# Attention and max-out FFN in one kernel: when value loads start, what follows them, and where two output blocks stand

## Chip, cores and metric

The kernel runs on one core of a Trainium2 chip, in one launch. Its time is the device time in microseconds, and the median of several runs is what is compared. A core has a matrix engine (PE), a vector engine (DVE), an activation engine (ACT), a general engine (POOL, GpSimd) and a queueing engine (SP). POOL and SP issue most transfers, which 16 DMA engines carry out.

## The reference

Eight batches of eight heads, 576 positions, head width 64. The inputs are float32.

```python
scores = scale * np.matmul(q, k.transpose(0, 1, 3, 2))
scores = scores + bias.transpose(2, 0, 1)[None, :, :, :]     # by distance, 32 buckets
attn = np.exp(scores - np.max(scores, axis=-1, keepdims=True))
attn = attn / (np.sum(attn, axis=-1, keepdims=True) + 1e-09)
x = np.matmul(attn, v)                                       # then to 4608 tokens x 512
h = np.maximum(np.maximum(x @ w1, x @ w2), x @ w3)           # 512 -> 768
return h @ w_out                                             # 768 -> 512
```

## The kernel before

**Tiles.** A batch b is worked off in four head pairs hp (HP = 4), so (b, hp) names a step. The 576 positions are four tiles of 128 (KT = 4) and a tail of 64. Scores are computed with keys on the partitions: `key_scores` (sc) gives one key tile against 512 queries, `left_keys_rows` (sct) the tail keys, and `left_queries` (scq) the tail queries. ACT takes the exponential of each (L776) into e4 or el. DVE multiplies a band around the diagonal by the exponential of the bias (L770; L856 and L869 for the tails). `attend_rows` then multiplies e4 and el by the values vx (main part) and vt (tail) on PE, into the tile a, one step later: the attention of (b, 3) is done in (b+1, 0), and that of (b+1, 0), the first to use batch b+1's values, in (b+1, 1).

**FFN between the scores.** From batch 4 on (ROWS) each step also runs one stage of the FFN of an earlier chunk of 512 tokens: in hp 2, hp 3 and the next batch's hp 0 a pair of gate blocks, and in hp 1 the outputs. Such a product is written as `pair`: `rows(False, c0, c1)` makes the first pass over blocks c0 to c1, `rows(True)` the second, with the partition halves exchanged. A pair of matmuls on the two halves runs side by side. In `outputs`, each of the six blocks (FCH = 6) of the first pass reads one block of hT. The last two blocks, 4 and 5, come from the third gate of the last gate pair, whose maximum (L518 on DVE) is what `largest` issues.

**Order.** `inorder` keeps instructions in program order on their engine, so the order on PE is that in which the Python code issues them. The output step's `run` sets: first half of sct, psp blocks, second half of sct, further psp blocks, the maximum, sc of key tile 3 (`more_scores`), bands, `left` (scq), and the rest. sc, sct and scq take turns in two PSUM buffers (pool ps_s): each waits until the exponential of the one two places before it is done. The second half of sct waits on a semaphore until the first half is through (`first_rows_end`, `behind_rows`).

**Transfers.** POOL issues the loads of q, k and v, which convert float32 to bfloat16 on the way. SP issues the transposes of q and k for the next batch (`transposes`, ten of them, q and k alternating through key tiles 0 to 3 and the tail), those of the attention's result x_sb into xT (L970, five at the end of a batch), and the stores of results. Each queue is worked in order. In step (b, 2) the program issues the loads of batch b+1's values (`load_v`: four vx, two vt) and then, for b from 2 to 5, those of batch b+2's q and k (`load_qk`: eight main parts, three tails); the buffers of both alternate. `go_behind(loads, ins)` makes each of these loads wait for an instruction `ins`, here the landing of a transpose: `turned_qk[b + 1, 1, t]` is that of key tile t of batch b+1, and t = KT is the tail. For b = 4 and up, values wait for t = KT and q and k for t = KT - 1.

Of the kernel before, what the change touches and what calls it, by code (L numbers as in the profile page):

```python
# [39 lines left out]
def kernel(  # L40
# [13 lines left out]
    B, H, S, D = q.shape  # L54
# [8 lines left out]
    KT = 4  # L63
# [14 lines left out]
    loads = ctx.enter_context(tc.tile_pool(name="loads", bufs=2))  # L78
# [36 lines left out]
    vx = [const.tile([P, KT, H, VW], BF16, name=f"vx{i}") for i in range(2)]  # L115
# [4 lines left out]
    def act_copy(out_, in_):  # L120
        return inorder(nc.scalar.activation(out=out_, in_=in_, func=ACTF.Copy))  # L121

    def dve_copy(out_, in_):
        return inorder(nc.vector.tensor_copy(out_, in_))  # L124

    def other_banks(later, earlier):

        for a in later:
            for b in earlier:
                tc.declare_no_dep(a.ins, b.ins, reason="they read different PSUM banks")  # L130
# [10 lines left out]
    def main_part(src, b):  # L141
        return src[b, :, 0 : KT * P, :].rearrange("h (t p) d -> p t h d", p=P)

    def tail_part(src, b, h0, h1, par):
        return src[b, h0 + par : h1 : 2, KT * P : S, :].rearrange("h p d -> p h d")

    def in_turn(b, load):
        return inorder(load)

    def load_main(src, b, h0, h1, dst, t0=0, t1=KT):  # L150
        x = main_part(src, b)
        return [
            in_turn(b, nc.gpsimd.dma_start(out=dst[:, t, h0:h1, :], in_=x[:, t, h0:h1, :])) for t in range(t0, t1)  # L153
        ]
# [5 lines left out]
    def load_q_tail(b):  # L160
        dst = qtail[b % 2][0 : S - KT * P].rearrange("p g (h d) -> p (g h) d", h=2)
        return in_turn(b, nc.gpsimd.dma_start(out=dst, in_=q[b, :, KT * P : S, :].rearrange("h p d -> p h d")))

    def k_diag(b, par, h0, h1):
        return diag(ktail[b % 2], par, h0, h1)
# [4 lines left out]
    def load_tail(src, b, h0, h1, dst):  # L170
        return [
            in_turn(b, nc.gpsimd.dma_start(out=dst(b, par, h0, h1), in_=tail_part(src, b, h0, h1, par)))
            for par in range(2)
        ]

    def load_qk(b, behind=None):

        loads = []
        for t in range(KT):
            for src, dst in zip((q, k), batch[b]):  # L180
                loads.append(in_turn(b, nc.gpsimd.dma_start(out=dst[:, t], in_=main_part(src, b)[:, t])))  # L181
        loads.append(load_q_tail(b))
        for par in range(2):
            load = nc.gpsimd.dma_start(out=k_diag(b, par, 0, H), in_=tail_part(k, b, 0, H, par))
            loads.append(in_turn(b, load))
        go_behind(loads, behind)

    def go_behind(loads, behind):

        for load in loads if behind else ():  # L190
            tc.add_manual_dep(
                load.ins, behind.ins.name,
                mybir.DependencyInfo(mybir.DependencyClass.Sync, mybir.DependencyReason.DATA),
                reason="these loads go behind the transposes in line",
            )

    def load_v(b, h0, h1, behind=None):
        loads = load_main(v, b, h0, h1, vx[b % 2][:, :, :, 0:D])
        go_behind(loads + load_tail(v, b, h0, h1, v_diag), behind)

# [139 lines left out]
    def pair(n, operands, pool, tag, w=CH):  # L342


        box = []

        def rows(swap, c0=0, c1=n):
            if not swap and c0 == 0:
                box.append(pool().tile([P, 2, CH], F32, tag=tag, name="psp"))
            made = []  # L350
            for c in range(c0, c1):
                for par in range(2):
                    i = par ^ swap
                    lhsT, rhs = operands[i](slice(64 * par, 64 * par + 64), c)
                    made.append(mm(
                        box[0][:, i, 0:w], lhsT=lhsT, rhs=rhs, start=not swap and c == 0, stop=swap and c == n - 1,
                    ))
            if swap:
                behind_rows(made[0], box[1])
            elif c1 == n:  # L360
                box.append(first_rows_end())

        return lambda: box[0][:, :, 0:w], rows

    def ffn(t0, nt, last, tiled=False):
# [172 lines left out]
        def columns(j, c0, c1):  # L538
            return lambda r, cf: (hT[r, cf * nt + j * P : cf * nt + j * P + P], wo_bf[r, cf, c0:c1])

        def osb_tile():
            return osbp.tile([P, d_model], F32, tag="osb", name="osb")

        def put_later(j, osb):
            r0 = t0 + j * P
            stores.append(lambda: inorder(nc.sync.dma_start(out=out[r0 : r0 + P, :], in_=osb[:])))

        def halves(j):
            ps, rows = pair(FCH, [columns(j, c, c + QS) for c in (0, QS)], lambda: ps_f, "ff", QS)

            def end():
                rows(True)

                def put():
                    osb = osb_tile()
                    dve_copy(osb[:].rearrange("p (i c) -> p i c", i=2), ps())
                    put_later(j, osb)
                return put
            return lambda: rows(False), end
# [28 lines left out]
        def outputs():  # L588
            ps0, rows0 = pair(FCH, [columns(j, 0, d_model) for j in range(2)], lambda: ps_a, "a")

            def end0():
                rows0(True)
                osb = osb_tile()
                first = act_copy(osb[:], ps0()[:, 0, :])
                put_later(0, osb)

                def put():
                    osb = osb_tile()
                    other_banks([dve_copy(osb[:], ps0()[:, 1, :])], [first])
                    put_later(1, osb)  # L600
                return put

            begin1, end1 = halves(2)

            def run(more_scores, left, ahead, largest, bands, keys):
                end_keys = keys()
                rows0(False, 0, 2)
                end_keys()
                rows0(False, 2, KT)
                largest()  # L610
                more_scores()
                bands()
                left()
                rows0(False, KT)
                begin1()
                put = end0()
                ahead()
                put()
                end1()()

            run.keys_late = True
            return run, lambda: halves(3)
# [143 lines left out]
    def times_band(hp, e4, t, lo, hi, put=lambda x: x):  # L766
        lo, hi = max(lo, P * t - P), min(hi, P * t + 2 * P)
        if lo < hi:
            c0, c1 = BAND - (hi - P * t + P), BAND - (lo - P * t + P)
            put(nc.vector.tensor_tensor(  # L770
                out=e4[:, t, :, lo:hi], in0=e4[:, t, :, lo:hi],
                in1=hank[:, 2 * hp : 2 * hp + 2, c0:c1][:, :, ::-1], op=ALU.mult,
            ))
# [86 lines left out]
    def left_queries(hp, qT, kT, el):  # L860

        sc = ps_s.tile([P, 2, CH], F32, tag="sc", name="scq")
        turn_left_queries(qT, kT, [sc[:, par, 0 : KT * 64] for par in range(2)])
        eq = el[:, S:].rearrange("p (t h q) -> p h t q", t=KT, h=2)
        return exp(eq, sc[:, :, 0 : KT * 64].rearrange("p h (t q) -> p h t q", t=KT))
# [7 lines left out]
    divided, turned_qk = {}, {}  # L873
# [161 lines left out]
    def bands(hp):  # L1035
        for t in range(KT):
            times_band(hp, first_e[hp], t, 0, QS, inorder)
# [40 lines left out]
    behind, begun = [], []  # L1078
    for hp in range(HP):
# [9 lines left out]
        def keys():  # L1089
            left_keys(hp, qT, kT, el, QS, S)  # L1090
# [57 lines left out]
    for b, hp in [(b, hp) for b in range(1, B) for hp in range(HP)]:  # L1148
# [61 lines left out]
        if rows:  # L1210
# [14 lines left out]
            def left():  # L1225
                left_queries(hp, qT, kT, el)
                times_band_left(hp, el)

            def ahead():
                n = HP * b + hp + 1  # L1230
                if n < HP * B:
                    begun.append(e_tiles())
                    key_scores(*(x[:, n % HP, :] for x in qk[n // HP]), begun[0][0], 0)
# [49 lines left out]
            rest.clear()  # L1283
            made, tail = ffn((b - 1) * CH, CH, False, [(b + (i + 2) // HP, (i + 2) % HP) >= ROWS for i in range(HP)])
        if hp == 2 and b + 1 < B:
            load_v(b + 1, 0, H, turned_qk[b + 1, 1, min(b, 2) if b < 4 else KT])
            if b == 1:
                load_last_weights(turned_qk[2, 1, KT - 1])
                batch[3] = load_tiles()
                load_qk(3, turned_qk[2, 1, KT - 1])  # L1290
        if hp == 2 and 1 < b < B - 2:
            batch[b + 2] = load_tiles()
            load_qk(b + 2, turned_qk[b + 1, 1, KT - 1])

        def queries():
            if not together:
# [68 lines left out]
```

## Time and profile before

| what | value |
|---|---|
| runs | 313.65, 313.75, 315.64 us; median 313.75 |
| profiled execution | 313.35 us |
| its span, first to last instruction | 311.6 us |
| PE busy | 300.2 us (96%) |
| DVE, ACT, POOL busy | 208.1, 202.1, 110.7 us |
| clock granted to PE | 0.998 |
| first output product of batches 4 to 7 | 134.3, 167.0, 199.3, 232.2 us |

A line of the timeline gives start and duration in us, engine, line, operation, output and inputs, shape and count; in brackets is the idle time before it and who ended it. PEld is PE's loading of weights, which overlaps its matmuls. "L107" is the helper that issues every matmul, so the tile names tell them apart: psp is a product of the FFN, sc, sct and scq are scores, a is attention times values. L153 and L172 load values, L181, L162 and L184 load q and k, and L701 transposes them.

### The profile page before, as it was taken

Reading aid. Unit: us, or ns where it says so; the run is one execution under the profiler, and the core shown is the slowest. Engines: PE = TensorE matmul, PEld = TensorE weight load, DVE = VectorE, ACT = ScalarE, POOL = GpSimd, SP = SyncE. Lnnn points to the kernel's source line nnn. Section 1 sums busy time; section 2 is a strip of 40 time slices with the busy share of each in tenths; the row PEclk is TensorE's granted clock in tenths of the full one; section 3 lists DMA queues with packets and bytes.
Section 4 is the critical chain, followed back from the end, with each engine's and each line's share of the span. In section 5 each row is a group of like instructions: output and inputs, shape, how many; then the busy total and the mean of one; then the engine's idle time right before and its main releaser. Section 6 shows DMA issues by size and latency. Waiting matters only on the chain.

```text
span 311.6 us, 10530 instructions
## 1 busy us (share of the span) xinstructions
PE 300.2 (96%) x4542; PEld 184.5 (59%) x4542; DVE 208.1 (67%) x475; ACT 202.1 (65%) x268; POOL 110.7 (36%) x147
## 2 busy tenths in 40 slices
PE   7989999999999999999999999999999999999995
PEld 2357777775555655667656766666657654444442
DVE  6389778776777776776776677766766675553552
ACT  3899988886777777767775867777767731122221
POOL 8978560952096106900295019600600000000000
PEclk9999999999999999999999999999999999999999
DMA  9999999999999999999999999999962015202003
GB/s 166 193 189 199 182 164 118 149 165 135 142 151 172 151 197 150 131 127 139 176 134 133 152 189 115 159 137 197 80 80 105 36 28 84 102 0 103 34 0 135
DMA packets 163950, 40.48 MB, mean 130 GB/s; under 512 B 153784, under 2 KB 159424, under 8 KB 163904
## 3 DMA queue, kind: packets, MB, share of 16 engines
q0 software_dynamic: 103840, 16.66, 81.8%
q1 hardware_dynamic: 58304, 22.69, 45.3%
q8 instruction: 35, 0.57, 0.8%
q10 hardware_dynamic: 1760, 0.47, 0.7%
q14 instruction: 11, 0.09, 0.1%
HBM read 35.39 MB, written 9.45 MB: 144 GB/s over the span
## 4 chain that ended last, share of the span: by engine, by line
PE 73%; DMA 16%; ACT 3%; issue 2%; SPq 2%; POOL 2%; DVE 1%; POOLq 0%; ACTq 0%; DVEq 0%
PE psp L107 26%; PE ps L107 18%; PE a L107 12%; PE sc L107 7%; PE pso L107 6%; DMA w_bf<-in_moe_w_dram 5%; DMA xT<-in_k_dram 3%; DMA vt<-in_v_dram 3%; PE sct L107 2%; SPq L701 1%; DMA kT<-ktail 1%; PE scq L107 1%; ACT e L776 1%; DMA hank<-w_dr 1%; DMA w_dr<-w_sb 1%
## 5 line engine op out<-in xcount | busy, mean ns | idle before, releaser
L776 ACT ACTIVATE e<-sc 128x1024 bf16<-128x1024 f32 x128 | 128.3, 1024 | 31.3 <-PE sc L107 28.1
L107 PEld LDWEIGHTS <-w_bf 64*128 64x128 bf16 (+1 forms) x1088 | 73.6, 95 | 56.5 <-issue 2.6
L107 PE MATMUL psp<-xT,w_bf 64*128 64x512 bf16 x736 | 91.5, 376 | 0.6 <-issue 0.6
L770 DVE TENSOR_TENSOR e<-e,hank 128x512 bf16<-128x512 bf16 (+2 forms) x136 | 62.3, 473 | 19.5 <-ACT e L776 19.0
L107 PE MATMUL ps<-xT,w_bf 128*128 128x512 bf16 (+1 forms) x352 | 65.6, 336 | 0.4 <-DMA w_bf<-in_moe_w_dram 0.4
L153 POOL DMA_DIRECT2D vx<-in_v_dram x28 | 24.6, 896 | 94.0 <-PE sc L107 69.3
L107 PE MATMUL sc<-qT,kT 64*128 64x256 bf16 (+1 forms) x384 | 48.5, 313 | 1.9 <-DVE kT L124 0.8
L107 PEld LDWEIGHTS <-kT 64*128 64x128 bf16 (+1 forms) x736 | 31.1, 95 | 27.6 <-issue 9.9
L107 PE MATMUL a<-vx,e 64*128 64x65 bf16 (+1 forms) x1536 | 44.9, 191 | 0.0
L107 PEld LDWEIGHTS <-e 64*128 64x128 bf16 (+1 forms) x1536 | 40.7, 95 | 4.7 <-issue 1.4
L107 PEld LDWEIGHTS <-hT 64*128 64x128 bf16 (+1 forms) x444 | 28.3, 95 | 17.5 <-issue 0.5
L107 PE MATMUL a<-vt,el 64*128 64x65 bf16 (+1 forms) x240 | 31.2, 201 | 1.4 <-DMA vt<-in_v_dram 1.0
L107 PEld LDWEIGHTS <-el 64*128 64x128 bf16 (+1 forms) x624 | 26.1, 95 | 8.7 <-issue 4.7
L776 ACT ACTIVATE el<-sct 128x576 bf16<-128x576 f32 (+2 forms) x36 | 21.6, 604 | 14.5 <-PE sct L107 14.1
L393 ACT ACTIVATE m<-ps 128x512 bf16<-128x512 f32 x14 | 8.4, 597 | 34.3 <-PE ps L107 34.3
L107 PE MATMUL psp<-wo_bf,hT 64*128 64x256 bf16 (+1 forms) x336 | 29.2, 307 | 0.0
L181 POOL DMA_DIRECT2D k_sb<-in_k_dram x24 | 22.5, 937 | 4.3 <-DMA wo_bf<-in_moe_w_out_dram 1.9
L181 POOL DMA_DIRECT2D q_sb<-in_q_dram x24 | 22.5, 936 | 2.9 <-DMA xT<-in_q_dram 1.5
L107 PE MATMUL pso<-wo_bf,hT 128*128 128x512 bf16 (+2 forms) x108 | 23.2, 367 | 0.0
L402 DVE TENSOR_TENSOR m<-ps,m 128x512 bf16<-128x512 f32 x14 | 9.7, 692 | 17.0 <-PE ps L107 17.0
L776 ACT ACTIVATE el<-scq 128x512 bf16<-128x512 f32 (+1 forms) x33 | 19.2, 585 | 2.2 <-PE scq L107 2.1
L121 ACT ACTIVATE m<-psp 128x1024 bf16<-128x1024 f32 (+1 forms) x22 | 18.2, 825 | 1.5 <-PE psp L107 1.1
(82 smaller groups left out, 285.9 us busy)
## 6 DMA issues: line engine op xcount, KB each, us to landing
out_dram<-osb SPq DMA_DIRECT2D x35, 256.0 KB, 3.5
vx<-in_v_dram POOLq DMA_DIRECT2D x28, 128.0 KB, 5.2
q_sb<-in_q_dram POOLq DMA_DIRECT2D x26, 128.0 KB, 8.4
k_sb<-in_k_dram POOLq DMA_DIRECT2D x24, 128.0 KB, 9.1
w_bf<-in_moe_w_dram POOLq DMA_DIRECT2D x3, 768.0 KB, 9.7
xT<-in_k_dram SPq DMA_DIRECT2D x6, 128.0 KB, 4.6
hank<-w_dr SPq DMA_DIRECT2D x2, 384.0 KB, 5.7
wo_bf<-in_moe_w_out_dram POOLq DMA_DIRECT2D x1, 768.0 KB, 8.5
```

The lines of the kernel that those rows point to most:

```text
L107: made = inorder(nc.tensor.matmul(*args, **kw))
L121: return inorder(nc.scalar.activation(out=out_, in_=in_, func=ACTF.Copy))
L153: in_turn(b, nc.gpsimd.dma_start(out=dst[:, t, h0:h1, :], in_=x[:, t, h0:h1, :])) for t in range(t0, t1)
L181: loads.append(in_turn(b, nc.gpsimd.dma_start(out=dst[:, t], in_=main_part(src, b)[:, t])))
L393: nc.scalar.activation(out=st[fb]["m0"][:], in_=ps0, func=ACTF.Copy)
L402: inorder(nc.vector.tensor_tensor(out=m[:], in0=ps1, in1=st[fb]["m0"][:], op=ALU.max))
L701: turned_qk[b, j, t] = inorder(nc.sync.dma_start_transpose(out=made[j][:, :, P * t : P * t + n], in_=src))
L770: put(nc.vector.tensor_tensor(out=e4[:, t, :, lo:hi], in0=e4[:, t, :, lo:hi], in1=hank[:, 2 * hp : 2 * hp + 2, c0:c1][:, :, ::-1], op=ALU. ...
L776: made = nc.scalar.activation(out=out_, in_=in_, func=ACTF.Exp, scale=inv_sqrt_d)
```

## The change

The values of batches 5, 6 and 7 (b from 4 to 6) wait for the transpose of the last main key tile instead of the key tail's. The loads of q and k of batches 6 and 7 (b = 4 and 5) wait for the last load of values, instead of that transpose. In the output steps of batches 4 to 7, one block instead of two stands between the halves of sct, and the first pass's blocks 4 and 5 stand ahead of the left-over queries (scq) instead of behind them. The order of instructions on ACT, DVE, SP and POOL stays as it was; on PE only the output steps differ.

```diff
     def load_v(b, h0, h1, behind=None):
-        loads = load_main(v, b, h0, h1, vx[b % 2][:, :, :, 0:D])
-        go_behind(loads + load_tail(v, b, h0, h1, v_diag), behind)
+        loads = load_main(v, b, h0, h1, vx[b % 2][:, :, :, 0:D]) + load_tail(v, b, h0, h1, v_diag)
+        go_behind(loads, behind)
+        return loads[-1]
...
                 end_keys = keys()
-                rows0(False, 0, 2)
+                rows0(False, 0, 1)
                 end_keys()
-                rows0(False, 2, KT)
+                rows0(False, 1, KT)
                 largest()
                 more_scores()
                 bands()
+                rows0(False, KT)
                 left()
-                rows0(False, KT)
                 begin1()
...
-            load_v(b + 1, 0, H, turned_qk[b + 1, 1, min(b, 2) if b < 4 else KT])
+            last_v = load_v(b + 1, 0, H, turned_qk[b + 1, 1, min(b, 2) if b < 4 else KT - 1])
...
-            load_qk(b + 2, turned_qk[b + 1, 1, KT - 1])
+            load_qk(b + 2, turned_qk[b + 1, 1, KT - 1] if b < 4 else last_v)
```

## Prediction

> **What bounds the kernel now.** First the page: which engine is full, and who ends the chain.
>
> ```profile
> span 311.6 us, 10530 instructions
> ...
> PE 300.2 (96%) x4542; PEld 184.5 (59%) x4542; DVE 208.1 (67%) x475; ACT 202.1 (65%) x268; POOL 110.7 (36%) x147
> ...
> PE 73%; DMA 16%; ACT 3%; issue 2%; SPq 2%; POOL 2%; DVE 1%; POOLq 0%; ACTq 0%; DVEq 0%
> ```
>
> PE is the bound: only what closes a hole in PE's stream, or opens one, moves the end. Then the timeline where batch 5's values are first used (start, duration, engine, operation):
>
> ```profile
> 161.52 1.04 PE L107 MATMUL psp<-xT,w_bf 64*128 64x512 bf16 x8
> ...
> 162.80 0.10 PEld L107 LDWEIGHTS <-el 64*128 64x128 bf16 x2 [0.73 <-DMA vt<-in_v_dram]
> ...
> 163.36 0.19 PE L107 MATMUL a<-vt,el 64*128 64x65 bf16 x1 [0.35 <-DMA vt<-in_v_dram]
> 163.36 0.18 PEld L107 LDWEIGHTS <-e 64*128 64x128 bf16 x8 [0.46 <-issue]
> ```
>
> At batch 6, where nothing is late, the same `e` weights come at 195.64, 0.87 us after their psp group (194.77). Here they should come at 162.39 and come at 163.36: a hole of 0.97 us. At batch 7 (psp 226.95, `e` weights 228.50) it is 0.68. Sum 1.65.
>
> What set it, by the POOL and SP timelines and the DMA view (last number: us from issue to landing):
>
> ```profile
> 146.65 1.22 SPq L701 DMA_TRANSPOSE kT<-k_sb  x1
> ...
> 149.26 1.21 SPq L701 DMA_TRANSPOSE kT<-ktail  x1
> ```
> ```profile
> 154.06 3.52 POOL L153 DMA_DIRECT2D vx<-in_v_dram  x4 [20.16 <-PE sc L107]
> 157.54 1.29 POOL L172 DMA_DIRECT2D vt<-in_v_dram  x2
> 158.76 0.95 POOL L181 DMA_DIRECT2D q_sb<-in_q_dram  x1
> ```
> ```profile
> kT<-k_sb SPq DMA_TRANSPOSE x1, 6.1
> ...
> kT<-ktail SPq DMA_TRANSPOSE x1, 4.2
> ```
>
> The wait on POOL is put down to a PE matmul, but 149.26 + 4.2 = 153.46 is when the tail keys land, 0.60 before vx: that transpose is the releaser (for batch 6 the wait names kT<-ktail outright). The last vt lands at 158.16 + 5.2 = 163.36, just when PE goes on.
>
> Last, the output pair of batch 5:
>
> ```profile
> 167.11 1.23 DVE L518 TENSOR_TENSOR hT<-psp,m 128x1024 bf16<-128x1024 f32 x1 [0.40 <-PE psp L107]
> ...
> 168.00 0.40 PE L107 MATMUL sc<-qT,kT 64*128 64x512 bf16 x2
> ...
> 168.55 0.29 PE L107 MATMUL scq<-qT,kT 64*128 64x64 bf16 x8 [0.15 <-ACT el L776]
> ...
> 168.63 2.09 PEld L107 LDWEIGHTS <-hT 64*128 64x128 bf16 x28
> ```
>
> A sc pair takes 0.22 (the chain's own figure), so PE is free at 168.22 and stands 0.33 us until the exponential of sct (167.84 + 0.65) gives scq its PSUM buffer. The other three output pairs: 0.26 (135.31 to 135.79), 0.33 (200.29, 200.84), 0.33 (233.14, 233.69). Sum 1.25.
>
> [...] POOL stands 20.16 us ahead of vx. So a q load that waits for the values holds every later POOL load. [...] SP's transposes share the engines. The trace fits: the last vt took 5.2 and 4.8 us where the x_sb transposes started together with vt (157.54, 222.93), 4.5 where they came later (190.79). [...]
>
> **Part 1, values one step sooner (batches 5, 6, 7).** Six POOL issues move, same order, no instruction added. For batch 5 the wait ends with 146.65 + 6.1 = 152.75 instead of 153.46: 0.71 sooner. Last vt at 162.65 against 162.39 wanted: 0.26 of the hole stays, 0.71 is won. For batch 7 the main keys' landing isn't printed; it lies between q's (210.07 + 5.1 = 215.17) and the query tail's (212.73 + 3.2 = 215.93). I take 215.6, so vx at 216.2 instead of 219.50: 3.3 sooner, all of 0.68 won, 2.6 to spare. For batch 6, 178.23 + 6.3 = 184.53 instead of 185.15, but no hole to win: the last vt lands at about 194.3 (second vt issue about 189.8, plus 4.5), wanted at 195.64.
>
> **Part 2, q and k behind the values (batches 6 and 7).** Eleven POOL issues now wait until the last vt has landed. For batch 6's q and k: first issue at about 162.65 + 0.3 = 162.9 instead of 158.76, 4.15 later. Nobody else waits on POOL; who waits is SP, for the transposes. Their cover in the trace of before, as landing (issue plus its time to landing) against transpose start: q0 163.96/164.91, k0 166.15/166.25, q1 167.3/167.56, k1 168.8/168.87, q2 171.05/172.11, k2 172.4/173.43, q3 173.8/176.40, k3 176.05/178.23. The first four have 0.1 to 0.9 us: no cover. So q0 is transposed at about 168.0, 3.1 late. Then the rest follows at SP's 1.3 us each: k0 169.4, q1 170.8, k1 172.2, q2 173.6, k2 175.0, three stores (1.5), q3 177.9, k3 179.2. The loss shrinks from 3.1 to 1.0 because SP's 3.15 us transpose (168.87), a place where the DMA engines were behind, should shrink to about 1.3. If it doesn't, k3 is 2.8 late. Landing 179.2 + 6.3 = 185.5, vx at 186.1: 0.4 later than 185.71 (range -0.6 to +2.2). Slack was 1.3 and PE arrives about 0.9 sooner, so 0.4 is left: a new hole of 0 to 1.8, taken as 0.3.
> For batch 7's q and k the delay is 194.7 + 0.3 - 190.42 = 4.6; cover was 198.18 - 195.6 = 2.6, so q0 is 2.0 late; but three stores at 207.67 stood for osb until 209.98, which takes most of it up. vx stays at 216.2 to 218.2, wanted before about 219.50 - 0.68 - 0.9 = 217.9: 0.1 lost. Keys and queries themselves: ahead() of batch 6 needs q0 to q3 at 186.76, which land 176.40 + 6.1 = 182.5; 1.5 late is covered.
> Sum of 1 and 2: -0.71 - 0.68 + 0.3 + 0.1 = -1.0.
>
> **Part 3, the output blocks (four output pairs).** One psp pair instead of two between the two halves of sct: the first half ends 166.89 + 0.30 = 167.19, the second may start at 167.23; with 0.05 for the semaphore 0.02 is lost, 0.1 in all. Sct is then done 0.22 sooner, so scq's buffer is free by about 168.3. In the hole come psp pairs 4 and 5; but these read hT blocks that L518 writes until 168.34, plus 0.05 (a DVE end at 171.93, weight load at 171.98). Today scq's wait hides that. New hole 168.22 to 168.39: 0.17. The others: 135.64, 200.63 and 233.48 give 0.16, 0.17, 0.17; sum 0.67. scq then ends about 169.15, before ACT is free for it (169.35). Won: 1.25 - 0.67 - 0.1 = 0.48. Bounds: if the matmul needs a further 0.1 after the late weights, 0.1; if DVE were never late, 1.15. I take 0.45: the wait is the same kind as the one at 171.98.
>
> **Sum.** 313.35 (profiled execution: span 311.6 and 1.75 around it) - 1.0 - 0.45 = 311.9. The median of the runs is 313.75, 0.4 above; there: 312.3.
>
> **Rivals.**
> (a) The stall is handed on: late q and k make batch 6's values late, a hole of about 1 us where there was none. For: four transposes without cover. Against: SP's and the DMA's own stalls may absorb it. Gain 0 to 0.7: 313.3.
> (b) Everything works, DVE included: -1.65 - 0.9: 311.2. Against: L518's end at 168.34.
> (c) Slower. Loop: values land, q and k load, transposes, values of the next batch: 9 + 5 + 13.3 (q0 to k3 as now) + 6.3 + 0.6 = 34.2 us against PE's batch of about 32.3 (195.64 - 163.36). It decides when batch 6's k3 is transposed after about 181.0 instead of 178.23: then vx after 187.9, and the new hole passes 1.85, which eats parts 1 and 3. At 183: about 315.5. For: the DMA share is full until 177. Against: it takes the whole 3.1 us plus the old stalls.
> (d) No effect of the load edit, if SP's queue sets all: part 3 alone, 313.3; counted with (a).
>
> **How the numbers follow.** Forecast (gain 0.8 to 2.2) 0.57; (a) and (d) 0.22; (b) 0.10; (c) 0.11. Predicted 312.3; its own range 311.5 to 313.0. The 8 in 10 range: below, (b) with the bounds of part 3, 311.0; above, (a) to its end and the beginning of (c), 314.1. Over 1% (3.1 us, about what a measurement of this kernel can tell) is more than all holes named (1.65 + 1.25): faster 0.04. Slower by over 1% is only the far end of (c): 0.04. Within: 0.92.
>
> **What would show it.** vx of batch 5 at about 153.35, its hole near 0.3; q load about 4 us after vt; batch 6's k3 transpose near 179 (right) or past 181 (c); at batch 6 a vt wait under 0.5; none at batch 7; in output pairs hT weights waiting for L518 for 0.17, and scq waiting for nobody. Wrong if the first transposes keep their time, or if the hT wait is absent.

## The result, and the profile after

The change: 313.24 us, median of 22 runs (311.48 to 319.41), against 314.15 us for the kernel before, measured beside it (22 runs); ratio 0.9967, 95% interval 0.9945 to 0.9989. That is 0.9 us less. The ratio leaves out a kernel's slow runs, those over 1.5% above its fastest. Measured once more (e9 below) the ratio was 1.0004, 0.9977 to 1.0030. So the gain is small, and the second measurement alone doesn't tell it from none. The forecast was 312.3 us, 1.45 less than the 313.75 known then. A gain of that size lies inside the first interval (0.3 to 1.7 us) and outside the second (0.7 us at most).

The profiled execution took 312.26 us. Its page, the lines that answer to those of before:

```profile
span 310.5 us, 10532 instructions
...
PE 298.9 (96%) x4542; PEld 182.5 (59%) x4542; DVE 207.7 (67%) x475; ACT 202.4 (65%) x268; POOL 110.9 (36%) x147
...
PE 89%; ACT 5%; DMA 2%; issue 1%; DVE 1%; ACTq 1%; DVEq 0%
```

DMA falls from 16% of the chain that ended last (50 us) to 2%. Only 14 us of these 50 belong to this part: the last vt of batches 5 and 7 (5.16 and 4.85 us) and batch 7's key tail (4.03). None of the three stands in the chain any more. Nearly all the rest lies ahead of 43 us, in loads that the change doesn't touch. The timeline at the first use of batch 5's values:

```profile
160.84 1.04 PE L107 MATMUL psp<-xT,w_bf 64*128 64x512 bf16 x8
...
161.49 0.11 PEld L107 LDWEIGHTS <-el 64*128 64x128 bf16 x2
161.71 0.21 PE L107 MATMUL a<-vt,el 64*128 64x65 bf16 x2
161.71 0.20 PEld L107 LDWEIGHTS <-e 64*128 64x128 bf16 x8
```

The `e` weights come 0.87 us after their psp group: the hole of 0.97 is gone. SP's and POOL's timelines and the landings of the main keys and the key tail show why (what was L701 is L702 here, and L518 is L519):

```profile
145.76 1.22 SPq L702 DMA_TRANSPOSE kT<-k_sb  x1
147.06 2.00 SPq L702 DMA_TRANSPOSE qT<-qtail  x1
149.17 1.21 SPq L702 DMA_TRANSPOSE kT<-ktail  x1
```
```profile
150.21 3.53 POOL L153 DMA_DIRECT2D vx<-in_v_dram  x4 [18.70 <-PE psp L107]
153.70 1.29 POOL L172 DMA_DIRECT2D vt<-in_v_dram  x2
159.56 0.90 POOL L181 DMA_DIRECT2D q_sb<-in_q_dram  x1 [4.57 <-DMA vt<-in_v_dram]
```
```profile
kT<-k_sb SPq DMA_TRANSPOSE x1, 3.9
...
kT<-ktail SPq DMA_TRANSPOSE x1, 2.4
```

The main keys land at 145.76 + 3.9 = 149.66, and vx follows 0.55 later, at 150.21: 3.85 us sooner than in the trace of before. About half of that is the new wait. The key tail, for which vx waited before, lands at 149.17 + 2.4 = 151.57, 1.9 us after the main keys, where the forecast had 0.71; the query tail's transpose, 2.00 us on SP here, kept it back. The other half is that SP's transposes landed sooner in this execution (the main keys in 3.9 us instead of 6.1), with the same loads as before up to there. And q waits 4.57 us for the last vt, as the edit says; the ten loads of q and k queued behind it on POOL start after it, from 160.44 to 169.08 us.

The output step of batch 5:

```profile
165.47 1.23 DVE L519 TENSOR_TENSOR hT<-psp,m 128x1024 bf16<-128x1024 f32 x1 [0.40 <-PE psp L107]
...
166.38 0.40 PE L107 MATMUL sc<-qT,kT 64*128 64x512 bf16 x2
...
166.75 0.12 PEld L107 LDWEIGHTS <-hT 64*128 64x128 bf16 x4 [0.47 <-DVE hT L519]
166.76 0.61 PE L107 MATMUL psp<-wo_bf,hT 64*128 64x512 bf16 x4
...
167.20 0.28 PE L107 MATMUL scq<-qT,kT 64*128 64x64 bf16 x8
```

scq waits for nobody now; block 4 waits for L519, which ends at 166.70. The two matmuls of the sc pair, on the two halves, start 0.02 us apart and take 0.38 each; from one free pair to the next it is 0.22 (psp at 165.95 and 166.17 in this trace). So PE is free at 166.38 + 0.22 = 166.60 and goes on at 166.76: a gap of 0.16 instead of 0.33.

And one thing that nobody had forecast, in the same trace at batch 6:

```profile
207.02 1.67 PE L107 MATMUL psp<-xT,w_bf 64*128 64x512 bf16 x13
...
210.02 0.11 PEld L107 LDWEIGHTS <-w_bf 64*128 64x128 bf16 x3 [1.84 <-issue]
210.03 0.60 PE L107 MATMUL psp<-xT,w_bf 64*128 64x512 bf16 x3 [1.34 <-issue]
```

In the middle of sixteen equal matmuls on data that are long there, PE stands 1.34 us, put down to "issue", that is to nothing the profile shows. In the trace of before the same place has 0.19:

```profile
208.73 1.67 PE L107 MATMUL psp<-xT,w_bf 64*128 64x512 bf16 x13
210.59 0.60 PE L107 MATMUL psp<-xT,w_bf 64*128 64x512 bf16 x3 [0.19 <-issue]
```

A step can be summed up by the time from its first sct matmul to the next step's. From batch 4 on, the shortest lengths that appear again and again are 7.36, 7.80, 9.75 and, for the output step, 6.68 before and 6.54 after. What a step has above them is hole (us, one profiled execution each):

| kernel | first use of values, batches 5, 6, 7 | four output steps | all other steps, sum of holes |
|---|---|---|---|
| before | 0.96, 0, 0.67 | 6.80, 6.68, 6.69, 6.68 | 1.31 |
| the change | 0, 0, 0 | 6.54, 6.53, 6.54, 6.53 | 2.94 |

So in this pair of executions 1.63 was won at the values and 0.7 in the output steps, and 1.63 lost in the steps between, 1.16 of it at the place above. A further 0.4 lies before 117 us, where both kernels run the same work.

### The profile page after: what moved, and what is told of

The parts are those of the page before. It is cut to its first block, busy times and chain, and to the rows that moved or that the text cites. A ratio compares the mean times of both kernels' runs of the same rounds, so it can differ in the third digit from the quotient of the medians.

```text
span 310.5 us, 10532 instructions
## 1 busy us (share of the span) xinstructions
PE 298.9 (96%) x4542; PEld 182.5 (59%) x4542; DVE 207.7 (67%) x475; ACT 202.4 (65%) x268; POOL 110.9 (36%) x147
## 4 chain that ended last, share of the span: by engine, by line
PE 89%; ACT 5%; DMA 2%; issue 1%; DVE 1%; ACTq 1%; DVEq 0%
PE psp L107 34%; PE ps L107 19%; PE a L107 14%; PE sc L107 9%; PE pso L107 6%; ACT e L777 4%; PE sct L107 2%; PE scq L107 2%; PE tp L111 1%; DMA xT<-in_q_dram 1%; DMA out_dram<-osb 1%; ACT el L777 1%; ACTq L213 1%; PE xp L111 0%; DVE k_sb L124 0%
## 5 line engine op out<-in xcount | busy, mean ns | idle before, releaser
L107 PEld LDWEIGHTS <-hT 64*128 64x128 bf16 (+1 forms) x444 | 26.9, 95 | 19.4 <-DVE hT L519 1.9
L519 DVE TENSOR_TENSOR hT<-psp,m 128x1024 bf16<-128x1024 f32 x12 | 14.7, 1225 | 6.9 <-PE psp L107 6.9
```

Of the source, the lines that this page charges most:

```text
L107: made = inorder(nc.tensor.matmul(*args, **kw))
L519: return lambda: inorder(nc.vector.tensor_tensor(out=hT[:, fb * CH : fb * CH + 2 * CH].rearrange("p (i t) -> p i t", i=2), in0=ps2(), in1= ...
```

## The experiments

Twelve runs. "The hold" below is the second edit, q and k waiting for the last load of values; a value hole is one at the first use of a batch's values, and "other holes" are those of the table's last column. The times of one kernel scatter by 1 us and more from run to run, so a ratio stands with its interval, and the traces say what is in it. All kernels are edits of before or of the change.

**e1: both load edits alone.** Output steps as before.

> Both load edits, output steps as before. Theory: the holes at the first use of batch 5's and batch 7's values (0.97 and 0.68 us before) are gone, no new one at batch 6; the four gaps ahead of scq (0.26 to 0.33 each) stay. Ratio about 0.996 (1.2 us less). If the delayed q and k loads cost PE time elsewhere (the 1.3 us hole inside a psp group of batch 6 that the changed kernel's trace shows, put down to nothing, 'issue'), that hole is here too. Rival, the gain comes from the output steps: ratio 1.000, and the trace shows value holes that are replaced by others.

Measured: 313.27 us, ratio 0.9984 (0.9957 to 1.0011). Value holes 0, 0.09, 0.01; the gaps ahead of scq stayed (6.61 to 6.69 a step); other holes 3.30, of which 2.02 in the step with the psp group, more than in the change. So the mechanism of the values is right, and the ratio doesn't show it.

**e2: the output steps alone.**

> Output steps of the change, loads as before. Theory: the value holes stay (0.97 at batch 5, 0.68 at batch 7, give or take 0.3 with the run), each output step is 0.14 us shorter, 0.55 in all, ratio about 0.998. The hole inside batch 6's psp group should be the 0.2 us of before, not 1.3. Rival, the output steps carry the whole gain: ratio 0.9965.

Measured: 314.44 us, ratio 0.9992 (0.9967 to 1.0017). Output steps 6.53 to 6.54, as expected. But the expected value holes weren't in this trace (0, 0.01, 0.01), although vx started as late as before (153.97): PE was 1.3 us later than in the trace of before (118.14 against 116.87 us at the same step). What had made it late was a value hole too: at 99.5 us it stood 1.63 us for the values of batch 3, whose loads no edit touches. The value holes are a race between PE and a chain of transfers, not a constant. The hole inside the psp group was 0.91 (1.28 in the whole step, 0.56 in before), not the 0.2 expected: it doesn't need late q and k.

**e3: the values sooner, q and k not held back.**

```diff
-            load_qk(b + 2, turned_qk[b + 1, 1, KT - 1] if b < 4 else last_v)
+            load_qk(b + 2, turned_qk[b + 1, 1, KT - 1])
```

(this and the output steps as before, against the change)

> Values wait for the last main key tile, q and k for that as well, right behind the values in POOL's queue as before. Theory (the sooner start is what closes the holes): vx starts 0.7 to 3.5 us sooner, the value holes fall to 0 to 0.3, ratio 0.996 or below, at least as good as both load edits together. Rival (q and k packets in flight slow the values, and holding them back is what helps): the holes stay at 0.6 or more and the ratio is near 0.999.

Measured: 311.87 us, ratio 0.9926 (0.9903 to 0.9949): 2.3 us less than before, and 0.0058 under both load edits together. That is more than the 1.63 of value holes in the trace of before; where the rest was won isn't shown. The trace, in POOL's timeline:

```profile
152.73 3.52 POOL L153 DMA_DIRECT2D vx<-in_v_dram  x4 [19.00 <-DMA kT<-k_sb]
156.21 1.29 POOL L172 DMA_DIRECT2D vt<-in_v_dram  x2
157.44 0.95 POOL L181 DMA_DIRECT2D q_sb<-in_q_dram  x1
```

The wait of vx now names the main keys. q follows vt at once, and still the value holes are 0, 0, 0: q and k behind the values don't slow them enough to open a hole. The rival falls. The two landings were closer than in the change: in this trace the main keys landed at 152.17 and the key tail at 152.72.

**e4: q and k held back, the values as late as before.**

> Values wait for the key tail as before, q and k wait for the last value load. Theory: values are no sooner, batch 5's hole stays near 0.9; q and k come about 4 us later, so batch 6's transposes and values come later, with a new hole of 0.5 to 2 us at batch 6 and perhaps 7: ratio 1.000 to 1.006. Rival (holding q and k back is what helps): the hole at batch 5 falls below 0.5, ratio 0.997.

Measured: 318.18 us (6 runs), ratio 1.0128 (1.0099 to 1.0157): 4 us slower, more than expected. Hole at batch 5 1.03, at batch 6 6.18. POOL's timeline, PE's weights, and stretches of PE's time with the granted clock (columns: stretch, length, busy time and count of PE, PEld, DVE, ACT, POOL, then the clock, DMA share, GB/s; the share counts the whole time of each packet that starts in the stretch, so it can pass 1):

```profile
188.00 3.53 POOL L153 DMA_DIRECT2D vx<-in_v_dram  x4 [16.10 <-PE sc L107]
191.48 1.29 POOL L172 DMA_DIRECT2D vt<-in_v_dram  x2
```
```profile
197.74 0.10 PEld L107 LDWEIGHTS <-el 64*128 64x128 bf16 x2 [3.62 <-DMA vt<-in_v_dram]
```
```profile
190.00:193.00 3.00, 3.00 (x30) 1.55 (x28) 2.12 (x5) 2.47 (x4) 2.78 (x4) 1.00 1.54 115
...
197.70:200.00 2.30, 2.25 (x64) 1.97 (x65) 0.00 (x0) 0.05 (x1) 1.57 (x2) 0.50 0.13 27
200.00:202.00 2.00, 2.00 (x43) 1.31 (x39) 0.90 (x2) 0.97 (x1) 2.00 (x4) 0.50 1.39 96
...
204.00:206.00 2.00, 1.85 (x28) 0.98 (x26) 1.62 (x3) 1.09 (x3) 2.00 (x3) 1.00 2.21 142
```

vx of batch 6 is 2.3 us later than before (188.00 against 185.71), so its values arrive 3 us after PE wants them. PE stands 3.1 us by the matmuls' own wait, and then works at half clock for some 6 us, which costs about 3 more: together the 6.18. This is the loop of rival (c), closed here by the key tail's transpose (183.47), and what the other edit of the change keeps away.

**e5: values sooner and the new output steps, q and k not held back.** The change with e3's line.

> The sooner values and the new output steps, but q and k wait for the last main key tile again, right behind the values in POOL's queue. Theory (holding q and k back costs about as much as it was meant to bring, and the other two parts add up): ratio 0.991 to 0.993, under the sooner values alone by 0.5 us or so. Rival (the two load edits belong together once the output steps are shorter): ratio about 0.997, that of the change.

Measured: 311.00 us, ratio 0.9892 (0.9860 to 0.9924) against a before of 314.99. Value holes 0, output steps 6.53 to 6.60. This is 0.0034 under e3, more than the output steps were expected to bring, and within the intervals; e10 is the same kernel again.

**e6: the same, with the last maximum in two instructions.**

```diff
+                    if fb + 2 == n_fb:
+                        return lambda: [inorder(nc.vector.tensor_tensor(
+                            out=block(fb + i), in0=ps2()[:, i, :], in1=m[0][:, i, :], op=ALU.max,
+                        )) for i in range(2)]
...
-                rows0(False, KT)
+                rows0(False, KT, KT + 1)
                 left()
+                rows0(False, KT + 1)
```

> As the kernel before it in this list, but the maximum of the last gate pair is made in two instructions, one for each block, and the left-over queries stand between output blocks 4 and 5. Theory (what remains of the gap in the output steps, 0.16 us each, is the wait for that maximum): block 4 no longer waits, scq covers the wait for block 5, each output step is 0.1 to 0.16 us shorter, 0.4 to 0.6 in all. Rival (the two instructions delay the DVE work behind them): no change or up to 0.3 us longer a step.

Measured: 309.50 us (6 runs), ratio 0.9848 (0.9800 to 0.9896). Output steps 6.37 and 6.36 in batches 6 and 7, 0.17 less; in batches 4 and 5 small issue holes fell in them (6.61, 6.81).

**e7: without batch 7's q and k loads.**

```diff
-            batch[b + 2] = load_tiles()
-            load_qk(b + 2, turned_qk[b + 1, 1, KT - 1] if b < 4 else last_v)
+            if b + 2 < B - 1:
+                batch[b + 2] = load_tiles()
+                load_qk(b + 2, turned_qk[b + 1, 1, KT - 1] if b < 4 else last_v)
+            else:
+                batch[b + 2] = batch[b]
```

> The change, without the eleven loads of batch 7's q and k: batch 7 is worked off with batch 5's q and k, so these loads (about 192 to 203 us) are left out. Theory (the hole inside a psp group of batch 6, at about 210 us, before the third-last pair, is PE waiting for its own instructions[...]): with the DMA engines emptier there, the hole of 1.3 to 1.65 us falls below 0.3. Rival (it has nothing to do with the DMA): it stays over 0.9.

Measured: 310.54 us (one run). PE at the same place:

```profile
207.04 0.39 PE L107 MATMUL sc<-qT,kT 64*128 64x512 bf16 x2
207.27 1.90 PE L107 MATMUL psp<-xT,w_bf 64*128 64x512 bf16 x16
209.00 0.19 PE L107 MATMUL scq<-qT,kT 64*128 64x64 bf16 x1
```

All sixteen in one piece: the step's hole is 0.01 instead of 1.72. The DMA engines, full until 208.6 us in the change, are idle for several stretches from 201 us on here. Alone this proves little: it is one execution, and e12, which has all the loads, has no hole at this place either.

**e8: the change with 32 more instructions on PE at the start.**

```diff
+    for _ in range(16):
+        mm(warm[:, 0:64], lhsT=zeros[:, 0:P], rhs=zeros[:, 0:64])
```

> The change, with sixteen more small matmuls at the start, where PE waits anyway: 32 more instructions on PE ahead of everything else. Theory (the unexplained holes sit at fixed places in PE's instruction stream, where a new block of instructions has to be there): the hole at about 210 us moves 32 instructions, or 16 matmuls, forward in the work: from the fourteenth matmul of the sixteen psp ones to the pair of sc ahead of these or just before that. Rival (it belongs to what these matmuls read or write): it stays at the fourteenth matmul.

Measured: 314.50 us (one run). PE, batch 6:

```profile
208.04 1.02 PE L107 MATMUL psp<-xT,w_bf 64*128 64x512 bf16 x7
210.55 0.39 PE L107 MATMUL psp<-xT,w_bf 64*128 64x512 bf16 x1 [1.49 <-issue]
210.56 0.60 PE L107 MATMUL sc<-qT,kT 64*128 64x512 bf16 x2
211.00 1.90 PE L107 MATMUL psp<-xT,w_bf 64*128 64x512 bf16 x16
```

The hole has left the sixteen psp and stands one matmul ahead of the sc pair: 13 + 2 + 1 = 16 matmuls, 32 instructions, earlier. So it belongs to the place in the instruction stream and not to the operands.

The other traces bear this out. In the ten that have 4542 matmul records, all issue holes of over 0.15 us after 30 us stand at six places: matmul 1113, 1878, 2771, 2899, 3410 (the one above) and 3538. From each to the next is a multiple of 128, to within three; with a weight load to every matmul, a multiple of 256 instructions. The page of the profile has a queue of kind "instruction" with 35 transfers of together 0.57 MB, 16,384 bytes each in the trace. The 4542 matmuls and as many weight loads of the page come to 260 of PE's instructions for each of these transfers, close to the spacing of the places. Whether all of them are PE's, the profile doesn't say.

The last of these transfers to start before matmul 3410 is the 26th. In the change it starts at 206.95 us, its packet takes 1.44 us, and PE goes on at 210.03, 3.1 us after the start. In all twelve traces with a hole at this place PE goes on 2.4 to 3.3 us after that start; in e12 and e7, which have none, PE comes there 3.1 and 4.5 us after it. The author's reading of these figures, which no view states, is that PE waits for its own instructions, and that the hole is what is missing of some 3 us between the transfer's start and PE's arrival. What fills these 3 us, and what makes the transfer start late, isn't shown. In e7, where it started earliest, the DMA share over the 4 us ahead was 0.46; in the other thirteen traces it was 1.3 to 2.1.

**e9 to e12: four kernels on one more chip.**

> The change itself once more, beside the next three on one chip. Theory: ratio about 0.9967 as before; value holes zero, and 0.5 to 2 us of holes in PE's stream that move with the instruction count. Rival (that trace was an accident): no hole over 0.3 us at the fourteenth matmul of batch 6's psp group.

> The change with q and k behind the last main key tile, not behind the values. Theory (holding q and k back pushes loads and transposes later, into the stretch where PE wants instruction blocks): 1.5 to 2.5 us under the change on the same chip, and its first transpose of batch 7's q follows x_sb's at once instead of 2 us later. Rival: the same as the change within 0.5 us.

> The change with the maximum in two instructions and scq between output blocks 4 and 5, q and k held back as in the change. Theory (two separate costs): 0.6 us or somewhat more under the change, still 1.5 us or more over the same with q and k not held back. Rival (the split alone makes the holes go): within 0.5 us of the next kernel.

> Sooner values, q and k not held back, maximum in two instructions: the fastest so far once more. Theory: ratio 0.985 to 0.989; output steps 6.36 to 6.40 us from the first half of sct to the next step's where no other hole falls in, against 6.54 with the maximum in one. Rival (its first measurement was luck): ratio 0.990 or above.

| | q and k held back | q and k right behind the values |
|---|---|---|
| maximum in one | the change (e9): 313.75, 1.0004 (0.9977 to 1.0030) | e10: 311.25, 0.9934 (0.9911 to 0.9958) |
| maximum in two | e11: 313.16, 0.9973 (0.9949 to 0.9998) | e12: 311.13, 0.9912 (0.9884 to 0.9940) |

Holding q and k back costs 0.0070 in one row and 0.0061 in the other, 1.9 to 2.2 us; the split brings 0.002 to 0.003, within the intervals (0.0044 between e5 and e6). e12 stays the fastest, but 0.9912 lies above the range expected and in the rival's: by that mark e6's 0.9848 was in part luck. And e10, e5's kernel, comes to 0.9934 instead of 0.9892, not under e3's 0.9926. So the shorter output steps are seen in every trace with this order, and their gain isn't shown by the ratios. e12's output step, where the last block's wait is now covered:

```profile
197.09 1.29 DVE L520 TENSOR_TENSOR hT<-psp,m 128x512 bf16<-128x512 f32 x2 [0.39 <-PE psp L107]
...
197.99 0.40 PE L107 MATMUL sc<-qT,kT 64*128 64x512 bf16 x2
...
198.21 0.40 PE L107 MATMUL psp<-wo_bf,hT 64*128 64x512 bf16 x2
198.43 0.30 PE L107 MATMUL scq<-qT,kT 64*128 64x64 bf16 x8
...
198.54 2.33 PE L107 MATMUL psp<-wo_bf,hT 64*128 64x512 bf16 x25
```

No gap: sc, block 4, scq, block 5 follow each other at 0.22, 0.22, 0.11 us.

The expectation for e10, that SP would take batch 7's q up sooner, held (195.95 us, against 197.13 in e9 and 199.91 in the first trace of the change), and its main keys are transposed at 209.75 against 212.31 and 212.40. But that the hold makes the issue holes larger is not shown. The other holes of one execution each are 2.94, 1.88, 3.30, 4.47 and 5.03 with it (the change, e9, e1, e8, e11) and 3.86, 2.29, 0.44, 2.63 and 0.05 without (e3, e5, e6, e10, e12), e7 aside. The averages, 3.5 and 1.9, differ by about what the hold costs, but the two sets overlap, and e11's is in part half clock.

## Why the prediction was right, and where its terms were off

The direction and range held: 313.24 lies between 311.0 and 314.1, the change within 1%. By its own steps:

- **Part 1, sooner values: mechanism right, term too small.** vx of batch 7 was put at 216.2 to 218.2, it came at 216.46, and the hole was gone. For batch 5 the head start was put at 0.71 with 0.26 of the hole left; it was 1.9 us, in an execution whose transposes landed sooner as well, with nothing left. The term was 1.39 for batches 5 and 7. Alone (e3) the part brought 2.3 us (1.6 to 3.0 by the interval). The term was read from the holes of one trace, and e2 shows that these are a race: with the same loads none was there.
- **Part 2, the hold on q and k: the term that was mis-sized.** It was put at 0.4 us; 1.8 (e1 against e3) and 2.2 (e9 against e10) were measured. Its path for batch 6 wasn't taken. The prediction had q0's transpose at about 168.0, 3.1 late, and named transposes that keep their time as a sign of being wrong. In the change it started at 164.23, 0.7 sooner than before: the last vt landed at 159.27 instead of the forecast 162.65, so that q was issued 0.8 later and not 4.15. In e4, where the values aren't sooner, it is at 168.06, the same hold makes batch 6's values 2.3 us late, and the step loses 6.2. For batch 7 the path held: SP took q up at 199.91, 1.7 late instead of 2.0. Batch 6's main keys were transposed at 178.41 (179.2 forecast), and its values (vx 184.14) came 1.6 us sooner than before, as PE did, so without a hole. Also left out was that a hole can cost more than itself, as in e4, where PE stood 3.1 us and lost about 3 more at a granted clock of 0.50.
- **Where the 2 us of the hold lie stays open.** The change's two profiled executions (312.26 and 311.61) are below their medians (313.24 and 313.75). Value holes of batches 6 and 7 add up to 0.3 in e9 and 0.1 in e1, and to none over 0.02 in the five kernels without the hold, so the margin is thin with it. One execution of e11 has 2.27 at batch 6's values; but at 319.05 us that execution is far above e11's median, and it also has 5.03 of other holes and 2.1 us of standing at 100.8, so it doesn't speak for the usual ones.
- **Part 3, the output steps: right to the hundredth in the trace.** A gap of 0.17 ahead of block 4 was forecast, 0.16 was found; 0.05 was put down to the semaphore between the halves of sct, and in the change the second half starts 0.06 after the first ends (165.26 + 0.30, 165.62). And 0.14 to 0.15 a step was won in e2 and the change, 0.56 to 0.7 in all against 0.48 worked out. The ratio of e2 can't tell it from none.
- **Not foreseen: holes at fixed places of PE's instruction stream.** The sum had only holes that name a cause. In before, 1.31 us of holes lay in other steps, "issue" among them; the change's trace has 2.94. They differ from one execution to the next (0.05 in e12, 5.03 in e11) and are in kernels with and without the hold. A sum over two traces that leaves them out is off by as much as the change is worth.
- **The sum.** The two misses go against each other: about 0.9 us more was won at the values, 1.4 to 1.8 more was lost by the hold. That the total came out inside the range is in part luck.
- **Rivals.** (a), the stall handed on, isn't in the traces of the change as a hole of 1 us at batch 6. By its gain the first measurement (0.9 us) is the forecast's (0.8 to 2.2), and the second (none) is (a)'s (0 to 0.7). (c) is real and is e4: vx at 188.00, past the 187.9 at which the loop was to decide; its hole was put at 1.85 us, and 3.1 of wait and about 3 of half clock came. (b) fell on the wait for L518, as argued.

## What to carry to other kernels

Here a load that stalled the bound engine was helped by shortening its own wait (e3: vx of batch 5 at 152.73 instead of 154.06, no value hole, 2.3 us less in all); making others wait for it could help only if they were in its way, and in e3, where they don't wait, the value holes are 0 as well. Where transfers feed transposes which feed the next transfers, holding one link back can come round again a batch later (e4: batch 6's q issued at 162.94 instead of 158.76, its vx at 188.00 instead of 185.71). And a wait swapped for another is worth the difference of the two ends (a gap of 0.16 for one of 0.33): look up when the next operand is ready (L518 here) before an order is changed, or split its producer (e6: 0.17 less in two of four steps).

## What the runs showed of the hardware

PE stood up to 2.14 us (e11) with nothing in the profile that it waits for, in the ten traces with 4542 matmul records at six places of its instruction stream, which are multiples of 256 instructions apart to within six. With 32 instructions more ahead of it the place of the largest lay 16 matmuls earlier in the work (e8). In the twelve traces with a hole there, PE goes on 2.4 to 3.3 us after a transfer of the queue "instruction" has started. In e7, with eleven loads fewer, that transfer started 4.5 us ahead of PE, in e12, with all of them, 3.1, and the step's hole is 0.01 in e7 and none stands at this place in e12. Such holes could be recognised in these traces: "issue" stands for their releaser, and in those ten they lie at the same six places.

After 3.1 us of standing, PE's granted clock was 0.50 from 197.7 to past 202 us in e4, and 1.00 again from 204. The hole thus cost 6.2. Two other traces don't go by the length of the hole. First e11, where the clock halved after less, then e5, where it didn't after as much (a line of PE's timeline and a stretch each, columns as in e4):

```profile
215.64 0.71 PE L107 MATMUL psp<-xT,w_bf 64*128 64x512 bf16 x3 [2.14 <-issue]
...
217.50:219.00 1.50, 1.50 (x28) 1.23 (x25) 0.27 (x1) 0.61 (x1) 0.00 (x0) 0.50 2.27 313
```
```profile
100.80 0.22 PE L107 MATMUL a<-vt,el 128*128 128x130 bf16 x1 [3.13 <-DMA vt<-in_v_dram]
...
100.80:103.00 2.20, 2.15 (x43) 1.73 (x45) 1.14 (x3) 0.00 (x0) 2.20 (x3) 1.00 2.14 144
```

In e11 the clock was 0.50 after 2.14 us of standing, in e5 it stayed 1.00 after 3.13, as long as e4's. So the length of a hole alone doesn't tell whether the clock halves; what decides isn't shown here.
